# Sums of squares of the heads: one float32 product replaced by two single float32r passes over a split of the squares into two parts

## The chip, the cores and the metric

The kernel runs on one core of a Trainium2 chip. The metric is the device time in microseconds (us) of one execution. All runs quoted here were of the state "fast"; most executions of one kernel on this case agree within about 0.3%, though those of the changed kernel spread by 0.5%. A profile comes from one execution, and its span is some 1.8 us shorter than the time of that run (the profiled execution of the kernel before is not one of the two timed below). The ratio of two kernels is the mean time of one kernel's runs over the mean time of the other's runs of the same rounds on the same chip, so it is not quite the ratio of the medians that stand beside it.

The engines go by short names: PE is TensorE, which multiplies matrices; DVE is VectorE, ACT is ScalarE, POOL is GpSimd. PE's products lie in banks of the memory PSUM, from which ACT and DVE read them here. The granted clock is the share of TensorE's full clock that the trace records. In the listings o is a product of the attention, tp the transposes of q, kv the product of k and v, ss the sum of squares, hp a product with w_in and op one with w_out. float32r is the language's second 32-bit float type; the prediction takes it for the reduced float32 of the Trainium skill.

## The reference

```python
kv  = np.einsum('bhsd,bhse->bhde', k, v)          # batch 8, heads 8, seq 576, head_dim 64
out = np.einsum('bhsd,bhde->bhse', q, kv)
rms = np.sqrt(np.mean(out * out, axis=-1, keepdims=True) + 1e-06)
out = out / rms * g_norm
x   = out.transpose(0, 2, 1, 3).reshape(4608, 512)
h   = x @ w_in                                     # 512 -> 2048
g   = np.maximum(h, 0) + np.log1p(np.exp(-np.abs(h)))
y   = g @ w_out                                    # 2048 -> 512
```

The weights come as float64, and the kernel converts them to float32 itself.

## The kernel before

Two heads share the 128 partitions. Per pair of heads the attention has three stages: `stage_turn` transposes q and forms kv, `stage_out` forms the rows o and their squares sq, and `stage_squares` sums the squares of a head with a product by a block of ones.

```python
def stage_out(u):
    ...
    for h in range(2):                                      # two halves of 288 tokens
        o = ps_a.tile([P, HS], F32, tag="a", name="o")
        nc.tensor.matmul(o, lhsT=kv_diag[u % 2], rhs=qT[:, h * HS:(h + 1) * HS], start=True, stop=True)
        sq = att.tile([P, HS], F32, tag="sq", name="sq")    # two buffers
        nc.scalar.activation(sq, o, func=AF.Square)
        nc.vector.tensor_scalar(out=x_of(b, p, h), in0=o, scalar1=g_col, scalar2=None, op0=ALU.mult)
        sqs[u, h] = sq

def stage_squares(u):
    b, p = divmod(u, NP)
    for h in range(2):
        ss = ps_a.tile([P, HS], F32, tag="a", name="ss")
        nc.tensor.matmul(ss, lhsT=block, rhs=sqs.pop((u, h)), start=True, stop=True)
        nc.vector.tensor_scalar(out=mss[b][:, h, p], in0=ss, scalar1=1.0 / D, scalar2=EPS, ...)
```

The dense part runs in "slots". A slot is one product hp of w_in with its softplus (Abs, Exp and Ln on ACT, four instructions on DVE), then what an agenda deals to this slot of the attention of a later batch, then in three slots of four a quarter of an output tile (op).

```python
for s in range(SLOTS):                        # 16 slots a block of 384 tokens, 12 blocks
    if n < n_blocks:
        mm1(n, s)                             # hp and softplus
    for f, a in agenda.pop(n * SLOTS + s, []):
        f(*a)                                 # squares of pair p-1 and turn of p, or out of p
    if n > 0 and s % 4 < 3:
        i, part = divmod(s // 4 * 3 + s % 4, PARTS)
        mm2(n - 1, i, part)                   # op
```

Of the kernel before, what the change touches and what calls it, by code (L numbers as in the profile page):

```python
# [7 lines left out]

F32 = mybir.dt.float32
U32 = mybir.dt.uint32  # L10
AF = mybir.ActivationFunctionType
ALU = mybir.AluOpType
PSUM = bass.MemoryType.PSUM
# [6 lines left out]
def kernel(  # L20
# [7 lines left out]
    moe_w_out: bass.AP,  # L28
    out: bass.AP,
):  # L30
    """Per batch and pair of heads: kv = k^T v, x^T = kv^T q^T (features on partitions, so that it is
    the moving operand of the next product), the mean of squares over a head by a product with a
    block of ones, which leaves it on every row of the head. Then per block of NT tokens:
    g = softplus(w_in^T x^T), out = g^T w_out. Products and sums are float32; weights that come as
    float64 (their bits in 64-bit integers) are rounded to it here. The attention of the batches
    ahead is dealt out over the slots of the block products."""
    nc = tc.nc
    B, H, S, D = q.shape
    d_model, d_ff = moe_w_in.shape
    n_tokens = out.shape[0]  # L40
    assert (B, H, S, D, d_model) == (8, 8, 576, 64, 512) and n_tokens == B * S
    NP = H // 2                      # pairs of heads
    KD, KF = d_model // P, d_ff // P
    J = 6                            # tokens on one partition of q, k and v
    R = S // J                       # partitions of q, k and v
    HS = S // 2                      # half of a batch's tokens: one bank of PSUM
    JH = J // 2
    NT = 384                         # tokens of a block
    SLOTS = KF
    GB = 2                           # batches whose x^T lies in one tile  # L50
    BPT = GB * S // NT               # blocks of such a tile
    n_blocks = n_tokens // NT

    ctx.enter_context(tc.manual_schedule())
# [10 lines left out]
    w_out_t = const.tile([P, KF, d_model], F32, name="w_out_t")  # L65
    ident = const.tile([P, P], F32, name="ident")
    block = const.tile([P, P], F32, name="block")
    g_col = const.tile([P, 1], F32, name="g_col")
    kv_diag = [const.tile([P, P], F32, name=f"kv_diag{i}") for i in range(2)]

# [2 lines left out]
    def load(u):  # L73
        if u >= B * NP:
            return
        b, p = divmod(u, NP)
        tiles = []
        for n, src in (("q", q), ("k", k), ("v", v)):
            # q and k are stationary operands: the pair's 128 features lie together for each j
            t = qkv.tile([R, 2, J, D] if n == "v" else [R, J, 2, D], F32, tag=n, name=f"{n}_t")  # L80
            pair = src[b, 2 * p:2 * p + 2].rearrange("h (r j) d -> r h j d", j=J)
            if n == "v":
                nc.sync.dma_start(out=t, in_=pair)
            else:
                for e in range(2):
                    nc.sync.dma_start(out=t[:, :, e], in_=pair[:, e])
            tiles.append(t)
        loaded[u] = tiles
# [3 lines left out]
    conv_pool = tc.tile_pool(name="conv", bufs=2)  # L92
    conv = conv_pool.__enter__()
    raws = {}
    CHUNKS = 2 * KF                  # a weight's columns (w_in) or rows (w_out) of one kf

    def weight(c):
        """DRAM and SBUF views of chunk c, d_model values on a partition."""
        kf = c % KF
        if c < KF:  # L100
            words = moe_w_in.bitcast(U32) if wide else moe_w_in
            n = words.shape[1] // KF
            return (words[:, kf * n:(kf + 1) * n].rearrange("(a p) f -> p a f", p=P),
                    w_in_t[:, :, kf * P:(kf + 1) * P])
        words = moe_w_out.bitcast(U32) if wide else moe_w_out
        return words[kf * P:(kf + 1) * P].rearrange("(a p) f -> p a f", p=P), w_out_t[:, kf:kf + 1]
# [10 lines left out]
            out=raws[c].rearrange("p n two -> p (n two)").rearrange("p (a f) -> p a f", a=src.shape[1]), in_=src)  # L117

    def convert(c):
        """float64 -> float32, from the words hi (sign, exponent, 20 bits of mantissa) and lo.  # L120

        t: hi's value in float32: the exponent's top bit and its low seven stay, the three between
        only tell the range. p: t's power of two with its sign. So the value is t + lo 2^-52 p,
        which one addition rounds. m is 1 inside float32's normal range, 0 below it, huge above."""
        if not wide:
            return
        raw = raws.pop(c)
        lo, hi = raw[:, :, 0], raw[:, :, 1]
        t, p, h = (conv.tile([P, d_model], U32, tag=n, name=f"c_{n}") for n in "tph")
        lf, m = (conv.tile([P, d_model], F32, tag=n, name=f"c_{n}") for n in ("lf", "m"))  # L130
        tf, pf = t.bitcast(F32), p.bitcast(F32)
        nc.scalar.activation(lf, lo, func=AF.Copy, scale=2.0 ** -52)  # L132
        nc.vector.tensor_scalar(out=h, in0=hi, scalar1=0x7FFFFFFF, scalar2=None, op0=ALU.bitwise_and)  # L133
        nc.vector.tensor_scalar(out=t, in0=hi, scalar1=3, scalar2=0x3FFFFFF8,
                                op0=ALU.logical_shift_left, op1=ALU.bitwise_and)
        nc.vector.scalar_tensor_tensor(out=t, in0=hi, scalar=0xC0000000, in1=t,
                                       op0=ALU.bitwise_and, op1=ALU.bitwise_or)
        nc.vector.tensor_scalar(out=p, in0=t, scalar1=0xFF800000, scalar2=None, op0=ALU.bitwise_and)
        nc.gpsimd.tensor_scalar(out=m, in0=h, scalar1=float((1023 + 128) << 20), scalar2=3e38,  # L139
                                op0=ALU.is_ge, op1=ALU.mult)  # L140
        nc.vector.scalar_tensor_tensor(out=m, in0=h, scalar=float((1023 - 126) << 20), in1=m,  # L141
                                       op0=ALU.is_ge, op1=ALU.add)
        nc.gpsimd.tensor_tensor(out=lf, in0=lf, in1=pf, op=ALU.mult)  # L143
        nc.gpsimd.tensor_tensor(out=lf, in0=lf, in1=tf, op=ALU.add)  # L144
        _, dst = weight(c)
        a = dst.shape[1]
        nc.gpsimd.tensor_tensor(out=dst, in0=lf.rearrange("p (a f) -> p a f", a=a),  # L147
                                in1=m.rearrange("p (a f) -> p a f", a=a), op=ALU.mult)
        fetch(c + 3)
# [14 lines left out]
        nc.vector.memset(t, 0.0)  # L164
    for e in range(2):
        nc.vector.memset(block[e * D:(e + 1) * D, e * D:(e + 1) * D], 1.0)

    xTs, mss = {}, {}
    qTs, sqs = {}, {}

    def stage_turn(u):
        """q^T and the block-diagonal kv of a pair of heads."""
        b, p = divmod(u, NP)
        if p == 0:
            mss[b] = att.tile([P, 2, NP, HS], F32, tag="ms", bufs=1, name="ms")
# [25 lines left out]
        return xTs[b // GB][:, p, c:c + HS]  # L201

    def stage_out(u):
        """The attention's rows times g, and their squares."""
        b, p = divmod(u, NP)
        qT = qTs.pop(u)
        for h in range(2):
            o = ps_a.tile([P, HS], F32, tag="a", name="o")
            nc.tensor.matmul(o, lhsT=kv_diag[u % 2], rhs=qT[:, h * HS:(h + 1) * HS], start=True, stop=True)  # L209
            sq = att.tile([P, HS], F32, tag="sq", name="sq")  # L210
            nc.scalar.activation(sq, o, func=AF.Square)
            nc.vector.tensor_scalar(out=x_of(b, p, h), in0=o, scalar1=g_col, scalar2=None, op0=ALU.mult)  # L212
            sqs[u, h] = sq

    def stage_squares(u):
        b, p = divmod(u, NP)
        for h in range(2):
            ss = ps_a.tile([P, HS], F32, tag="a", name="ss")
            nc.tensor.matmul(ss, lhsT=block, rhs=sqs.pop((u, h)), start=True, stop=True)  # L219
            nc.vector.tensor_scalar(out=mss[b][:, h, p], in0=ss, scalar1=1.0 / D, scalar2=EPS,  # L220
                                    op0=ALU.mult, op1=ALU.add)

# [13 lines left out]
    def mm1(n, kf):  # L236
# [5 lines left out]
        for kd in range(KD):  # L242
            nc.tensor.matmul(hp, lhsT=w_in_t[:, kd, kf * P:(kf + 1) * P], rhs=xT[:, kd, c:c + NT],  # L243
                             start=(kd == 0), stop=(kd == KD - 1))
        # softplus(h) = max(h, 0) + log1p(u), u = exp(-|h|);
        # log1p(u) = ln(w) + (u - (w - 1)) with w = 1 + u rounded, which keeps small u whole
        # once what the table gives for ln(1) is taken off.
        u = tmp.tile([P, NT], F32, tag="u", name="u")
        nc.scalar.activation(u, hp, func=AF.Abs)  # L249
        nc.scalar.activation(u, u, func=AF.Exp, scale=-1.0)  # L250
        ln = tmp.tile([P, NT], F32, tag="ln", name="ln")
        nc.scalar.activation(ln, u, func=AF.Ln, bias=1.0)  # L252
        w = tmp.tile([P, NT], F32, tag="w", name="w")
        nc.vector.tensor_scalar(out=w, in0=u, scalar1=1.0, scalar2=None, op0=ALU.add)  # L254
        nc.vector.scalar_tensor_tensor(out=w, in0=w, scalar=1.0, in1=u, op0=ALU.subtract, op1=ALU.subtract)  # L255
        nc.vector.scalar_tensor_tensor(out=ln, in0=hp, scalar=0.0, in1=ln, op0=ALU.max, op1=ALU.add)  # L256
        nc.vector.scalar_tensor_tensor(out=gs[n][:, kf], in0=ln, scalar=ln_one, in1=w,  # L257
                                       op0=ALU.subtract, op1=ALU.subtract)

    PARTS = 4                        # slots over which one tile of 128 tokens is summed  # L260

    def mm2(n, i, part):
        if part == 0:
# [8 lines left out]
            r0 = n * NT + i * P  # L272
            nc.sync.dma_start(out=out[r0:r0 + P], in_=ot)

    # the first batch
    for t in range(NP + 2):
        if t < NP:
            stage_turn(t)
# [7 lines left out]
        for p in range(NP):  # L286
            stage_norm(0, h, p)

    # the other batches, by slot
    agenda = {}  # L290

    def at(slot, f, *a):
        agenda.setdefault(slot, []).append((f, a))

    for b in range(1, B):
        # the slot where the first block that takes from batch b starts, less the slots of its work
        due = (b * S // NT) * SLOTS
        s0 = max(due - (28 if b % GB else 30), 0)
        for p in range(NP):
# [4 lines left out]
        for i in range(2 * NP):  # L304
            at(s0 + 2 * NP + (i + 1 if b > 1 else i), stage_norm, b, i // NP, i % NP)

    AHEAD = NP + 2                   # chunks of the weights that are ready before the first block
    for c in range(AHEAD, CHUNKS):
        at((c - AHEAD) * SLOTS // (CHUNKS - AHEAD), convert, c)

# [44 lines left out]
```

## Time and profile before

| | before |
|---|---|
| time, median of 2 runs | 1355.41 us (1354.22 to 1356.6) |
| span of the profiled run | 1353.7 us |
| PE, DVE, ACT busy | 1166.8, 775.3, 418.8 us |
| stretch bound by the conversion of the weights | about 34 to 306 us |
| stretch bound by PE | 306 us to the end |
| first product o after the conversion | 313.99 us |

The last line is a mark: everything before it is the first batch and the conversion, everything after it ("the rest") is bound by PE, 1353.7 - 314.0 = 1039.7 us.

### The profile page before, as it was taken

The page shows a single profiled execution, that of the slowest core. Times are in us where ns is not written, and L with a number is a line of the kernel's source. Part 1 is how long each engine was busy: PE and PEld are TensorE (multiplying, and loading weights), DVE is VectorE, ACT ScalarE, POOL GpSimd, SP SyncE. Part 2 cuts the span into 40 slices and gives each one's busy share as a digit, 9 for nine tenths or more (in the row PEclk, how much of TensorE's full clock was granted, in tenths as well). Part 3 has the DMA queues.
Part 4 walks back from the last instruction along what each step waited for, and adds up shares of the span by engine and source line. Part 5 has one row for each costly group of instructions (what it writes and reads, how often), then busy time and mean ns, then how long its engine had stood idle before and what let it go on. Part 6 is the DMA issues. An engine that isn't in the chain of part 4 may idle for free.

```text
span 1353.7 us, 10306 instructions
## 1 busy us (share of the span) xinstructions
PE 1166.8 (86%) x3520; PEld 642.1 (47%) x3520; DVE 775.3 (57%) x1254; ACT 418.8 (31%) x798; POOL 214.2 (16%) x134
## 2 busy tenths in 40 slices
PE   6164524259999999999999999999999999999998
PEld 4042312125555555555555555555555555555543
DVE  4888989885384476343674584335844754343320
ACT  2222222113433343333432433334233333233320
POOL 5658776770000000000000000000000000000000
PEclk8667766579999999999999999999999999999999
DMA  9324311102202200012012100121020000000000
GB/s 212 86 73 115 89 62 46 62 16 66 55 8 61 61 8 8 16 46 68 16 35 60 35 9 8 30 65 35 8 61 9 8 16 9 8 8 8 16 8 24
DMA packets 98582, 55.21 MB, mean 41 GB/s; under 512 B 77536, under 2 KB 91872, under 8 KB 98528
## 3 DMA queue, kind: packets, MB, share of 16 engines
q1 hardware_dynamic: 98528, 54.54, 14.9%
q8 instruction: 28, 0.46, 0.1%
q14 instruction: 26, 0.21, 0.0%
HBM read 45.09 MB, written 9.44 MB: 40 GB/s over the span
## 4 chain that ended last, share of the span: by engine, by line
PE 76%; DVE 10%; POOL 8%; ACT 3%; issue 1%; DMA 1%; SPq 1%; POOLq 0%; ACTq 0%
PE op L267 36%; PE hp L243 34%; POOL c_m L139 4%; PE kv L192 3%; DVE ms L229 2%; PE o L209 2%; DVE w L255 2%; DVE w L254 2%; POOL c_lf L143 2%; POOL c_lf L144 1%; DVE g L257 1%; DVE c_m L141 1%; ACT qT L187 1%; ACT u L250 1%; ACT u L249 1%
## 5 line engine op out<-in xcount | busy, mean ns | idle before, releaser
L243 PE MATMUL hp<-xT,w_in_t 128*128 128x384 f32 x1536 | 550.7, 507 | 111.3 <-DVE ln L256 85.2
L267 PE MATMUL op<-w_out_t,g 128*128 128x512 f32 x1152 | 516.1, 592 | 0.0
L243 PEld LDWEIGHTS hp<-xT,w_in_t 128*128 128x128 f32 x1536 | 303.7, 199 | 358.4 <-issue 98.6
L254 DVE TENSOR_SCALAR w<-u 128x384 f32<-128x384 f32 x192 | 85.9, 448 | 468.1 <-ACT u L250 468.1
L267 PEld LDWEIGHTS op<-w_out_t,g 128*128 128x128 f32 x1152 | 217.0, 190 | 238.1 <-issue 211.9
L249 ACT ACTIVATE u<-hp 128x384 f32<-128x384 f32 x192 | 93.9, 489 | 580.5 <-PE hp L243 580.4
L257 DVE SCALAR_TENSOR_TENSOR g<-ln,ln_one,w 128x384 f32<-128x384 f32 x192 | 124.9, 650 | 14.5 <-POOL w_out_t L147 0.7
L255 DVE SCALAR_TENSOR_TENSOR w<-w,u 128x384 f32<-128x384 f32 x192 | 122.3, 637 | 6.7
L229 DVE RECIPROCAL ms<-ms 128x288 f32<-128x288 f32 x64 | 124.5, 1945 | 2.2 <-ACT ms L224 2.2
L256 DVE SCALAR_TENSOR_TENSOR ln<-hp,ln 128x384 f32<-128x384 f32 x192 | 105.9, 551 | 0.9
L252 ACT ACTIVATE ln<-u 128x384 f32<-128x384 f32 x192 | 100.5, 524 | 6.1
L250 ACT ACTIVATE u<-u 128x384 f32<-128x384 f32 x192 | 100.4, 523 | 6.1
L139 POOL TENSOR_SCALAR c_m<-c_h 128x512 f32<-128x512 uint32 x32 | 70.4, 2201 | 81.7 <-DVE c_h L133 80.6
L192 PE MATMUL kv<-v_t,k_t 96*128 96x128 f32 x384 | 58.7, 310 | 21.6 <-ACT qT L187 16.2
L192 PEld LDWEIGHTS kv<-v_t,k_t 96*128 96x128 f32 x384 | 52.7, 217 | 26.6 <-ACT qT L187 20.6
L132 ACT ACTIVATE c_lf<-raw 128x512 f32<-128x512 uint32 x32 | 21.2, 667 | 127.3 <-POOL w_out_t L147 84.7
L209 PE MATMUL o<-qT,kv_diag 128*128 128x288 f32 x128 | 40.8, 445 | 21.1 <-DVE kv_diag L195 20.4
L143 POOL TENSOR_TENSOR c_lf<-c_lf,c_p 128x512 f32<-128x512 f32 x32 | 56.5, 1767 | 2.6
L271 ACT COPY ot<-op 128x512 f32<-128x512 f32 x36 | 21.1, 586 | 109.1 <-PE op L267 109.1
L184 PE MATMUL tp<-ident,q_t 96*128 96x96 f32 x192 | 24.3, 266 | 24.9 <-DVE xT L212 18.9
L209 PEld LDWEIGHTS o<-qT,kv_diag 128*128 128x128 f32 x128 | 25.8, 207 | 34.1 <-DVE kv_diag L195 22.3
L219 PE MATMUL ss<-sq,block 128*128 128x288 f32 x128 | 37.7, 419 | 4.4 <-DVE xT L212 2.9
(33 smaller groups left out, 469.9 us busy)
## 6 DMA issues: line engine op xcount, KB each, us to landing
q_t<-in_q_dram SPq DMA_DIRECT2D x64, 144.0 KB, 3.1
k_t<-in_k_dram SPq DMA_DIRECT2D x64, 144.0 KB, 3.5
v_t<-in_v_dram SPq DMA_DIRECT2D x32, 288.0 KB, 3.8
out_dram<-ot SPq DMA_DIRECT2D x36, 256.0 KB, 2.0
raw<-in_moe_w_in_dram SPq DMA_DIRECT2D x16, 512.0 KB, 4.1
raw<-in_moe_w_out_dram SPq DMA_DIRECT2D x16, 512.0 KB, 3.3
g_col<-in_g_norm_dram SPq DMA_DIRECT2D x2, 0.2 KB, 3.1
```

The source lines that it names most:

```text
L139: nc.gpsimd.tensor_scalar(out=m, in0=h, scalar1=float((1023 + 128) << 20), scalar2=3e38, op0=ALU.is_ge, op1=ALU.mult)
L192: nc.tensor.matmul(kv, lhsT=k_t[:, j].rearrange("r h d -> r (h d)"), rhs=v_t[:, :, j, :], start=(j == 0), stop=(j == J - 1))
L229: nc.vector.reciprocal(r, r)
L243: nc.tensor.matmul(hp, lhsT=w_in_t[:, kd, kf * P:(kf + 1) * P], rhs=xT[:, kd, c:c + NT], start=(kd == 0), stop=(kd == KD - 1))
L249: nc.scalar.activation(u, hp, func=AF.Abs)
L250: nc.scalar.activation(u, u, func=AF.Exp, scale=-1.0)
L252: nc.scalar.activation(ln, u, func=AF.Ln, bias=1.0)
L254: nc.vector.tensor_scalar(out=w, in0=u, scalar1=1.0, scalar2=None, op0=ALU.add)
L255: nc.vector.scalar_tensor_tensor(out=w, in0=w, scalar=1.0, in1=u, op0=ALU.subtract, op1=ALU.subtract)
L256: nc.vector.scalar_tensor_tensor(out=ln, in0=hp, scalar=0.0, in1=ln, op0=ALU.max, op1=ALU.add)
L257: nc.vector.scalar_tensor_tensor(out=gs[n][:, kf], in0=ln, scalar=ln_one, in1=w, op0=ALU.subtract, op1=ALU.subtract)
L267: nc.tensor.matmul(op, lhsT=gs[n][:, kf, i * P:(i + 1) * P], rhs=w_out_t[:, kf], start=(kf == 0), stop=(kf == KF - 1))
```

## The change

A pass is one run of the operand through PE; the prediction counts four for a float32 product and one for a float32r product. The change splits each square into hi, a slightly scaled copy that ACT writes as float32r, and lo, the rest (the square less hi), and sums both in single float32r passes into the same bank: two passes instead of four. To make room, sq and the softplus's w are cut to one buffer. With two buffers of sq and the rest of the change as it is, the program does not fit: the conversion's pool wants 32 KiB of each partition and finds 31.53.

```diff
+    block_r = const.tile([P, P], F32R, name="block_r")
 ...
+    nc.vector.tensor_copy(block_r, block)
 ... stage_out:
-            sq = att.tile([P, HS], F32, tag="sq", name="sq")
+            sq = att.tile([P, HS], F32, tag="sq", bufs=1, name="sq")
             nc.scalar.activation(sq, o, func=AF.Square)
             nc.vector.tensor_scalar(out=x_of(b, p, h), in0=o, ...)
-            sqs[u, h] = sq
+            hi = att.tile([P, HS], F32R, tag="hi", name="hi")
+            lo = att.tile([P, HS], F32R, tag="lo", name="lo")
+            nc.scalar.activation(hi, sq, func=AF.Copy, scale=1.0 - 2.0 ** -13)
+            nc.vector.tensor_tensor(out=lo, in0=sq, in1=hi.bitcast(F32), op=ALU.subtract)
+            sqs[u, h] = hi, lo
 ... stage_squares:
-            nc.tensor.matmul(ss, lhsT=block, rhs=sqs.pop((u, h)), start=True, stop=True)
+            for i, part in enumerate(sqs.pop((u, h))):
+                nc.tensor.matmul(ss, lhsT=block_r, rhs=part, start=(i == 0), stop=(i == 1))
 ... mm1:
-        w = tmp.tile([P, NT], F32, tag="w", name="w")
+        w = tmp.tile([P, NT], F32, tag="w", bufs=1, name="w")
```

The other lines of the diff define the name F32R and drop comments.

More of the change, by code (lines that the diff above doesn't have):

```diff
@@ L10 @@
 U32 = mybir.dt.uint32
+F32R = mybir.dt.float32r
 AF = mybir.ActivationFunctionType
```

## The prediction

> **What bounds the kernel now.** I read the page first, then a table of busy time by stretch, the waits, the chain that ended last, and the timeline of single slots. A "slot" is one turn of the kernel's inner loop: one product of w_in (8 records of hp), whatever attention work is dealt to it, and in three slots of four 8 records of the product with w_out (op).
>
> The page's strip of 40 slices (34 us each) shows two regimes. DVE and POOL are full and PE half empty, at a reduced granted clock, for the first eight or nine slices; after that PE is full and POOL is done.
>
> ```profile
> PE   6164524259999999999999999999999999999998
> DVE  4888989885384476343674584335844754343320
> POOL 5658776770000000000000000000000000000000
> PEclk8667766579999999999999999999999999999999
> ```
>
> The table by stretch puts numbers on it:
>
> ```profile
> core 0: us, PE busy (x) PEld busy (x) DVE busy (x) ACT busy (x) POOL busy (x), PEclk, DMA share, GB/s
> 34.00:306.00 272.00, 116.43 (x288) 65.97 (x289) 240.42 (x283) 61.98 (x109) 197.02 (x119) 0.67 0.24 68
> 306.00:1308.00 1002.00, 987.77 (x3048) 541.22 (x3046) 516.31 (x934) 345.29 (x666) 0.00 (x0) 1.00 0.10 28
> ```
>
> From 34 to 306 us the weights are converted; DVE (240 of 272 us) and POOL (197) take turns. From 306 to 1308 PE is busy 988 of 1002 us at full clock. The other 14 us are nearly all one wait, in the waits of that stretch: 18 kv products that wait for a copy of q^T on ScalarE.
>
> ```profile
> PE kv L192 <- ACT qT L187: 14.2, 18, 0.8
> ```
>
> So in the long stretch only PE's own path counts: time taken out of PE helps unless such a wait eats it, and time added on ACT or DVE hurts only where PE comes to wait for it.
>
> **What the Trainium skill says.** (1) "FP8 and Floating Point Precision", section TensorE Precision Notes: true float32 takes four passes, reduced float32 is read cut to about 22 bits. With "TensorE: Matmul & The Clock Gate", section Back-to-back issue gap (N/2.4 + 2.5 ns warm), a float32 product of 288 columns should take 4 x 122.5 = 490 ns. The trace agrees: two ss products begin at 443.79 and the next work at 444.76, 0.97 us. (A float32 product leaves two records, so 128 records are 64 products.) (2) "PSUM — Partial Sum Buffer", section on bank collisions: a scheduler adds a dependency between any two instructions of different engines on one bank, reads included. The trace agrees: the scaling xT (DVE) waits for the square sq (ACT) of the same bank, though it does not use it. (3) "SBUF — State Buffer", section two separate sides: DVE instructions with two SBUF inputs and GpSimd exclude each other. The trace agrees in that the two-input product xT (L231) took 0.88 us once beside POOL work and 0.46 us without.
>
> **The change part by part.** Removed: 64 float32 products ss (128 records, four passes). Added: 128 float32r products, which I take as one pass each; 64 copies hi on ACT; 64 subtractions lo on DVE; one small copy at the start, hidden. Moved: sq has one buffer instead of two, so the square of a pair's second half waits until lo of the first half has read sq. In the order of the built program the scaling of the second half waits for that square. So what ran as sq, sq on ACT beside x, x on DVE becomes a zigzag: x0, lo0 (DVE), sq1 (ACT), then hi1 (ACT) beside x1 (DVE), then lo1 (DVE), and only then the last of the four ss passes. The single buffer of w costs nothing: DVE alone writes and reads it, in order.
>
> Passes: 4 x 122.5 = 0.49 us per pair of heads instead of 0.97, so 0.48 saved per pair, on paper 32 x 0.48 = 15 us. Most of it is not paid out. Here is a slot from the timeline (start us, duration, engine, line):
>
> ```profile
> 440.24 1.13 PE L209 MATMUL o<-qT,kv_diag 128*128 128x288 f32 x4
> 441.21 2.74 PE L243 MATMUL hp<-xT,w_in_t 128*128 128x384 f32 x8
> 441.95 0.69 ACT L211 ACTIVATE sq<-o 128x288 f32<-128x288 f32 x2
> 443.63 0.94 DVE L212 TENSOR_SCALAR xT<-o,g_col 128x288 f32<-128x288 f32 x2
> 443.79 1.13 PE L219 MATMUL ss<-sq,block 128*128 128x288 f32 x4
> 443.99 0.49 ACT L249 ACTIVATE u<-hp 128x384 f32<-128x384 f32 x1 [1.35 <-PE hp L243]
> 444.76 0.66 PE L184 MATMUL tp<-ident,q_t 96*128 96x96 f32 x6
> 445.50 0.66 ACT L187 COPY qT<-tp 128x288 f32<-128x288 f32 x1
> 446.21 1.60 PE L192 MATMUL kv<-v_t,k_t 96*128 96x128 f32 x12 [0.79 <-ACT qT L187]
> ```
>
> Between the products o and ss stands only one hp (2.58 us), as the slot has no op. Today sq is long ready at 443.79, and ss starts without a wait. I listed o and what follows for all 24 pairs after 306 us: 12 have hp alone between o and ss ("short"), 12 have op and hp, 6.0 us ("long"). 9 of the short and 9 of the long are followed by transposes and kv (the 18 waits above); 3 of each are the last of their batch and are followed by op.
>
> A short pair, from the start of o as zero. DVE reaches x0 at 3.39 as now (443.63), its interval is 0.47. lo0: a DVE tensor_tensor of this shape, L231, takes 0.46, so it ends at 4.32. sq1 on ACT: 0.41 alone in this trace, with 0.05 for the hand-over, 4.37 to 4.78. Then x1 on DVE 4.82 to 5.33. hi1 on ACT: 0.44, from Exp of 384 columns at 0.52 less 96/1.2 ns, so to 5.25. lo1 5.29 to 5.75. The last ss pass ends near 5.95, against 4.52 now: PE waits, and goes on about 1.45 us later, the shorter passes already counted. If kv follows, ACT decides: Abs of this slot starts after hi1 at 5.16 instead of 3.75, so Abs, Exp, Ln and the q^T copy, and kv with them, come 1.4 us later. Both ways about +1.43: 12 x 1.43 = +17.2 us.
>
> A long pair: the same zigzag ends near 5.75, and ss begins 6.98 after o, so nothing waits. Where kv follows, the 0.48 us only lengthens the wait for the q^T copy, as that copy stands behind Abs, Exp and Ln of the slot's hp and not behind ss: gain 0. Where op follows: 3 x -0.48 = -1.4 us. After 306 us together +15.8.
>
> In the conversion, DVE is in the chain around every scaling of batch 1, as the chain in order of time shows:
>
> ```profile
> 93.44 0.94 DVE g L257
> 94.39 0.85 DVE xT L212 x2
> 95.66 1.77 POOL c_m L139
> ```
>
> The two scalings (0.93 us in the timeline) become x0, lo0, the hole for sq1, x1, lo1: 0.46 + 0.46 + 0.46 + 0.46 + 0.46 = 2.3 us, so +1.37 for each of four pairs, +5.5 us, handed on to POOL, which stands idle for c_h there. For batch 0, the first two pairs hide behind loads and a present wait of sq for ss (a buffer of sq), which the change removes; the later two have some slack beside POOL. I put +1.5 on it. Conversion +7.
>
> Sum: 1355.4 + 15.8 + 7.0 = 1378 us, 1.7% slower.
>
> **The rivals.** (a) The gain is paid out: PE is the bound, half of ss goes, and DVE and ACT have room (57% and 31% busy). Then 24 x 0.48 = 11.5 us fall away, at best 1344. For it speaks the full PE row; against it the 18 waits for q^T, which ss does not end, and the 12 short pairs. (b) The zigzag does not reach PE, because the short pairs' hp is long enough. That needs lo1 before 3.55, and x0 alone ends at 3.86. Only the conversion's cost would stay: about 1361. (c) The delays are larger: lo is locked out by GpSimd work in the conversion, each hand-over costs 0.1 us more, the weight loads of the single passes (0.19 us in the trace) stand bare after a wait, or ACT's delay reaches the next slots. 0.5 us more per short pair and 1 us more per pair in the conversion give 1392. (d) float32r is no cheaper than float32. No row of this trace tells. It would add 0.49 us to the 15 pairs at most that are not held by q^T: up to 1386.
>
> **Range and chances.** The zigzag's steps are durations of this trace, so rival (a) is unlikely. The least certain terms are the conversion (0 to 14 us) and the waits per short pair (1.0 to 1.9). That gives 1366 to 1390. The line of 2% lies at 1382.5, 4.5 us above my number, with some 8 us of spread. Faster 0.03, same 0.66, slower 0.31.
>
> **What would show it.** Each step has its place in the new profile: ss records 128 of about 0.12 us spacing, PE busy down by some 15 us; new waits of PE at ss for lo (DVE) in exactly 12 slots after 306 us, or of kv for q^T grown from 0.8 to about 2 us in the 9 short ones and to about 1.3 in the long ones; sq1 about 0.8 us behind sq0's end or more, waiting for lo; DVE up by 64 x 0.46 = 29 us, ACT by 28; the PE-bound stretch beginning at about 313 instead of 306. It would be wrong if the short pairs start kv on time, if the passes are not single, or if the conversion ends where it did.

## The result, and the profile after

The changed kernel took 1389.0 us (median of 2 runs, 1385.43 and 1392.57) against 1355.41: ratio 1.0248, 95% interval 1.0218 to 1.0278. The profiled run had a span of 1383.7 us. In a later job the same kernel took 1386.77 us (4 runs), ratio 1.0227. So it is slower by somewhat more than 2%.

The table of busy time by stretch, kernel after. The columns are start and end, length, busy us of each engine with its instruction count, the mean granted clock, the DMA share and GB/s.

```profile
320.00:1320.00 1000.00, 969.13 (x2971) 528.71 (x2970) 526.47 (x960) 360.22 (x699) 0.00 (x0) 0.99 0.10 28
```

From 320 to 1320 us PE is idle for 31 of 1000 us, where it was idle for 14 of 1002 before. And the granted clock is 0.99, where it was 1.00: a small digit that turns out to matter. The waits from 312 us on, kernel after (who waited, for whom, us in total, times, longest):

```profile
ACT sq L214 <- DVE lo L220: 42.9, 24, 1.8
...
PE kv L195 <- ACT qT L190: 17.1, 18, 1.2
...
PE ss L228 <- ACT hi L219: 6.9, 12, 0.6
...
PE ss L228 <- DVE lo L220: 5.8, 12, 0.5
```

The three waits of PE are the old one for the q^T copy and two new ones, each in 12 places: the 12 short pairs. (kv does not read q^T. In the built program 22 of the 32 kv are given the PSUM bank of the transposes before them, so they wait until ACT has copied these out.) The first line is the zigzag: 24 times ACT stands for 1.8 us with the square of the second half, until lo of the first half has read the only buffer. A short pair in the timeline of the kernel after (start us, duration, engine, line, and in brackets the idle time before):

```profile
451.84 1.13 PE L212 MATMUL o<-qT,kv_diag 128*128 128x288 f32 x4
...
453.54 0.39 ACT L214 ACTIVATE sq<-o 128x288 f32<-128x288 f32 x1
453.97 0.44 ACT L219 ACTIVATE hi<-sq 128x288 fp32r<-128x288 f32 x1
...
455.23 0.51 DVE L215 TENSOR_SCALAR xT<-o,g_col 128x288 f32<-128x288 f32 x1
455.66 0.45 DVE L220 TENSOR_TENSOR lo<-sq,hi 128x288 fp32r<-128x288 f32 x1
...
456.20 0.41 ACT L214 ACTIVATE sq<-o 128x288 f32<-128x288 f32 x1 [1.79 <-DVE lo L220]
456.64 0.44 ACT L219 ACTIVATE hi<-sq 128x288 fp32r<-128x288 f32 x1
456.65 0.52 DVE L215 TENSOR_SCALAR xT<-o,g_col 128x288 f32<-128x288 f32 x1 [0.54 <-ACT sq L214]
456.99 0.47 ACT L258 ACTIVATE u<-hp 128x384 f32<-128x384 f32 x1
457.12 0.46 DVE L220 TENSOR_TENSOR lo<-sq,hi 128x288 fp32r<-128x288 f32 x1
...
457.63 0.40 PE L228 MATMUL ss<-lo,block_r 128*128 128x288 f32 x1
...
457.87 0.66 PE L187 MATMUL tp<-ident,q_t 96*128 96x96 f32 x6
...
458.49 0.66 ACT L190 COPY qT<-tp 128x288 f32<-128x288 f32 x1
...
459.20 1.60 PE L195 MATMUL kv<-v_t,k_t 96*128 96x128 f32 x12 [0.67 <-ACT qT L190]
```

Read it against the slot of before in the prediction, with o as zero. The last lo ends at 5.74 us (predicted 5.75), Abs of this slot starts at 5.15 instead of 3.75 (5.16), and kv starts at 7.36 instead of 5.97 (7.41). The steps fell where they were put.

What was not foreseen is in the following lines: the same table for 3.4 us stretches around another short pair of the kernel after, whose o started at 353.25.

```profile
358.00:361.41 3.41, 2.10 (x15) 1.70 (x16) 2.80 (x6) 2.47 (x6) 0.00 (x0) 1.00 0.01 2
361.41:364.80 3.39, 3.39 (x11) 2.03 (x10) 1.67 (x5) 0.21 (x1) 0.00 (x0) 0.53 0.58 132
364.80:368.20 3.40, 3.40 (x10) 1.61 (x9) 0.00 (x0) 0.00 (x0) 0.00 (x0) 0.96 0.49 131
```

After a stretch in which PE was busy only 2.10 of 3.41 us, the granted clock is halved for 3.41 us although PE is full again, and those 3.41 us of work lose about 1.7 us. The trace's record of the clock has four such half-clock windows in the PE-bound rest of this run, and none in that of the kernel before. Four of them are 6.8 us.

The sum for the profiled runs is then closed: the first o after the conversion came at 321.58 us instead of 313.99 (+7.6), and the rest took 1062.1 us instead of 1039.7 (+22.4). Of the 22.4, the short pairs are 9 x 1.39 (kv) + 3 x 1.51 (the op after ss, which starts 6.03 instead of 4.52 us after o) = +17.0, the three long pairs before op are 3 x -0.44 = -1.3, and the four half-clock windows are +6.8: together 22.5.

### The profile page after: what moved, and what is told of

It is laid out like the page before. It is cut to its first block, busy times and chain, and to the rows that moved or that the text cites. A ratio compares the mean times of both kernels' runs of the same rounds, so it can differ in the third digit from the quotient of the medians.

```text
span 1383.7 us, 10559 instructions
## 1 busy us (share of the span) xinstructions
PE 1179.8 (85%) x3520; PEld 647.0 (47%) x3520; DVE 801.6 (58%) x1319; ACT 447.7 (32%) x862; POOL 213.8 (15%) x134
## 4 chain that ended last, share of the span: by engine, by line
PE 72%; DVE 13%; POOL 8%; ACT 5%; issue 1%; DMA 1%; SPq 1%; ACTq 0%; POOLq 0%
PE op L276 36%; PE hp L252 31%; POOL c_m L141 4%; PE kv L195 4%; DVE w L264 2%; DVE ms L238 2%; DVE w L263 2%; DVE g L266 2%; POOL c_lf L145 1%; ACT u L259 1%; PE o L212 1%; ACT u L258 1%; DVE ln L265 1%; POOL c_lf L146 1%; DVE c_m L143 1%
## 5 line engine op out<-in xcount | busy, mean ns | idle before, releaser
L195 PE MATMUL kv<-v_t,k_t 96*128 96x128 f32 x384 | 64.1, 330 | 25.1 <-ACT qT L190 20.8
L195 PEld LDWEIGHTS kv<-v_t,k_t 96*128 96x128 f32 x384 | 57.5, 234 | 30.2 <-ACT qT L190 25.2
L214 ACT ACTIVATE sq<-o 128x288 f32<-128x288 f32 x64 | 25.8, 404 | 107.0 <-DVE lo L220 96.1
L228 PE MATMUL ss<-lo,block_r 128*128 128x288 f32 x64 | 24.0, 381 | 41.1 <-DVE lo L220 39.9
L212 PE MATMUL o<-qT,kv_diag 128*128 128x288 f32 x128 | 42.2, 456 | 15.7 <-DVE kv_diag L198 15.1
L215 DVE TENSOR_SCALAR xT<-o,g_col 128x288 f32<-128x288 f32 x64 | 32.9, 514 | 18.2 <-ACT sq L214 18.1
```

The lines of the kernel that those rows point to most:

```text
L195: nc.tensor.matmul(kv, lhsT=k_t[:, j].rearrange("r h d -> r (h d)"), rhs=v_t[:, :, j, :], start=(j == 0), stop=(j == J - 1))
```

## The experiments

The theory: the time is lost because the one buffer of sq strings the two halves of a pair into a zigzag between DVE and ACT. In the conversion it lengthens DVE's chain; after it, it holds up PE directly (ss for lo) and through ACT (kv for the q^T copy behind the delayed hi), in the 12 short pairs only; and the holes it makes in PE bring half-clock windows on top. The rivals: the added work of hi and lo costs the time by itself; PE's wait for lo is all of it; the single passes are dear; the half-clock windows are accidental.

For all runs, the marks read from the PE timeline and the clock record of the one profiled execution:

| kernel | ratio to before (95%) | first o after conversion, us | rest, us | half-clock windows in the rest |
|---|---|---|---|---|
| before | 1 | 314.0 | 1039.7 | 0 |
| after | 1.0248 (1.0218 to 1.0278) | 321.6 | 1062.1 | 4 |
| e1 two buffers of sq | 1.0091 (1.0076 to 1.0106) | 319.0 | 1047.5 | 1 |
| e2 after, op first | 0.9895 (0.9878 to 0.9911) | 322.2 | 1017.8 | 0 |
| e3 before, op first | 0.9863 (0.9848 to 0.9877) | 314.1 | 1021.2 | 0 |
| e4 one pass | 0.9970 (0.9955 to 0.9985) | 314.1 | 1037.1 | 1 |
| e5 after again | 1.0227 (1.0213 to 1.0241) | 320.2 | 1063.7 | 5 |
| e6 after, waits filled | 1.0159 (1.0145 to 1.0173) | 322.9 | 1055.4 | 0 |
| e7 op first, two buffers | 0.9823 (0.9810 to 0.9837) | 320.0 | 1011.0 | 0 |
| e8 as e7, split late only | 0.9789 (0.9775 to 0.9802) | 314.3 | 1011.1 | 0 |
| e9 split in batches 0, 1 only | 1.0056 (1.0039 to 1.0073) | 323.5 | 1039.7 | 0 |
| e10 split in batches 2 to 7 only | 1.0178 (1.0162 to 1.0193) | 312.1 | 1063.7 | 5 |
| e11 work of hi and lo, unused | 1.0043 (1.0026 to 1.0059) | 319.3 | 1039.7 | 0 |
| e12 PE does not wait for lo | 1.0243 (1.0222 to 1.0264) | 321.7 | 1066.9 | 6, two of them double |

The medians were: e1 1368.19, e2 1341.76, e3 1337.12, e4 1352.05, e5 1386.77, e6 1377.68, e7 1332.58, e8 1327.70, e9 1363.99, e10 1379.86, e11 1361.02, e12 1389.65 us, each of 4 runs (e6 of 5), beside medians of before of 1355.65 (e1 to e4), 1356.38 (e5 to e8) and 1355.35 us (e9 to e12).

### e9 and e10: the two terms of the sum, each alone

```diff
+            split = b < 2          # e9;  b >= 2 in e10
 ... where not split: sq takes a buffer of the tag "hi" (two of them), no lo,
 ... and ss is the float32 product with block, as before
```

> The change in batches 0 and 1 alone (their work is done in the conversion stretch); batches 2 to 7 keep the float32 product of one square. Theory: the conversion's term of the sum by itself, +7 to 8 us, ratio 1.0055; the first o after the conversion near 321.5 us instead of 314.0. Rival (DVE has room there, 1 us in 9 idle): below 1.002.

> The change in batches 2 to 7 alone; batches 0 and 1 keep the float32 product. Theory: the PE-bound term by itself, 16 us and some half-clock windows (4 to 8 of 1.7 us): ratio 1.016 to 1.022, and the conversion ends at 314 us as before. With e9 it makes up the whole. Rival (the passes saved on PE show): below 1.01.

e9 gave 1.0056, and its rest is 1039.7 us, to the digit that of before: the split of the early batches costs only in the conversion. e10 gave 1.0178, with the conversion over at 312.1 us and all of the loss in the rest. Together they are 2.3%, as much as the whole in e5. So about a quarter of the loss is the conversion's and three quarters are PE's.

### e11: the added work without the waits

```diff
 ... before, with
+            hi = att.tile(...); lo = att.tile(...)
+            nc.scalar.activation(hi, sq, func=AF.Copy, scale=1.0 - 2.0 ** -13)
+            nc.vector.tensor_tensor(out=lo, in0=sq, in1=hi.bitcast(F32), op=ALU.subtract)
             sqs[u, h] = sq         # still the operand of the float32 product; two buffers
```

> The kernel before, with hi and lo computed and then not used: ACT and DVE do all the added work, sq has two buffers, PE still multiplies sq in float32 and waits for no hi or lo. Theory: PE does not see it after 306 us (ss waits for sq alone), only the conversion pays 4 to 5 us: ratio 1.0035. Rival (the work is the cost): about 1.02.

It gave 1.0043, and the rest is again 1039.7 us. In the rest, ACT and DVE do all that the change adds, and PE's time does not move by a tenth of a microsecond. The rival "the work is the cost" falls for the PE-bound part. In the conversion the work does cost, 5.3 us by the first o. This kernel also has the single buffer of w, which thereby is cleared.

### e1: two buffers of sq

```diff
-            sq = att.tile([P, HS], F32, tag="sq", bufs=1, name="sq")
+            sq = att.tile([P, HS], F32, tag="sq", name="sq")
 ... room: no tile "block"; the ones are set in kv_diag[0], copied to block_r, and cleared
```

> The change with two buffers of sq again (room made by building the block of ones in a tile that is zeroed afterwards). Theory (zigzag over one buffer): sq1 and hi1 no longer wait for lo0, so ACT's Abs starts on time in the short pairs; only the four DVE steps x0, lo0, x1, lo1 in a row remain, lo1 ending near 5.25 us after o. Then kv comes 0.6 us later than before in the 9 short pairs with kv, and PE 1.0 us later in the 3 without: about +7 us after 306 us, +5 us in the conversion, ratio to before about 1.009 to 1.013. Rival (the added work of hi and lo costs the time, not the wait): as the change, 1.025.

It gave 1.0091. In the short pairs kv starts 6.53 us after o (predicted 6.6; 7.36 with one buffer) and the op after ss at 5.37 (6.03). More than half of the loss goes away with one buffer of 1152 bytes per partition: of the 1.39 us by which kv came late in these pairs, the missing buffer made 0.83. What stays is the row of four DVE steps, which still ends after PE arrives.

### e12: PE spared the wait for lo, ACT not

```diff
-            for i, part in enumerate(sqs.pop((u, h))):
+            hi, lo = sqs.pop((u, h))
+            for i, part in enumerate((hi, hi)):
```

> The change with hi multiplied twice instead of hi and lo (the sums come out nearly double, so the result is wrong by a factor of about 0.7, on purpose): lo is computed, and sq1 still waits for it through the one buffer, but PE does not. Theory: in the 9 short pairs followed by kv nothing is gained, as kv waits for the q^T copy that stands behind the delayed sq1 and hi1 on ACT, and 0.4 us in the 3 others: ratio 1.022 to 1.024. Rival (PE's wait for lo is the cost): about 1.008.

The result is wrong as intended (relative error 0.21). The ratio stayed at 1.0243: kv still starts 7.36 us after o. In the pair whose o started at 451.95:

```profile
459.31 2.15 PE L195 MATMUL kv<-v_t,k_t 96*128 96x128 f32 x12 [1.02 <-ACT qT L190]
```

PE's direct wait for lo, the line that catches the eye in the list of waits, is not what sets the time in the nine pairs followed by kv. There it is ACT, held up by the zigzag, that delivers the q^T copy late. This run also had more half-clock windows than the others, six, two of them of double length.

### e4: what the saved passes are worth

```diff
 ... before, with
-            sq = att.tile([P, HS], F32, tag="sq", name="sq")
+            sq = att.tile([P, HS], F32R, tag="sq", name="sq")
-            nc.tensor.matmul(ss, lhsT=block, rhs=sqs.pop((u, h)), start=True, stop=True)
+            nc.tensor.matmul(ss, lhsT=block_r, rhs=sqs.pop((u, h)), start=True, stop=True)
```

> The kernel before with the square written as float32r and a single pass (no hi, no lo; coarser, so the result may be off by some 1e-4). PE saves 0.72 us per pair. Theory: of the 24 pairs after 306 us the 18 that are followed by kv give it back as a longer wait for the q^T copy, so 6 x 0.72 = 4 us, ratio 0.997. Rival (the saved passes are paid out in full and only the split's work costs): 24 x 0.72 = 17 us, ratio 0.987.

It gave 0.9970, as the theory said, and within the accepted error, though it multiplies squares written as float32r and has no lo. A short pair in the PE timeline of this kernel:

```profile
439.66 1.13 PE L213 MATMUL o<-qT,kv_diag 128*128 128x288 f32 x4
...
442.91 0.72 PE L223 MATMUL ss<-sq,block_r 128*128 128x288 f32 x2
443.61 0.89 PE L188 MATMUL tp<-ident,q_t 96*128 96x96 f32 x6
445.63 1.60 PE L196 MATMUL kv<-v_t,k_t 96*128 96x128 f32 x12 [1.12 <-ACT qT L191]
```

The transposes start 3.95 us after o instead of 4.52, and kv starts at 5.97 as before: the wait for the q^T copy has grown by what ss gave up. The rest of the profiled run, 1037.1 us, contains one half-clock window, at 1011.94 us after such a pair; without its 1.67 us it would be 4.3 us shorter than before, the 6 x 0.72 of the theory. A window can thus appear without any zigzag, after a pair whose only added hole is the longer wait for the q^T copy. So even a quarter of the passes at no added work is worth 0.3% in this schedule.

### e5 and e6: the half-clock windows

e5 is the change unaltered. e6 puts useless passes where PE waits, in the 12 short pairs:

```diff
             hi, lo = sqs.pop((u, h))
+            for _ in range((4 if h == 0 else 2) if short else 0):
+                nc.tensor.matmul(ss, lhsT=block_r, rhs=hi, start=True, stop=True)
+            for _ in range(4 if short and h == 0 else 1):
                 nc.tensor.matmul(ss, lhsT=block_r, rhs=hi, start=True, stop=False)
                 nc.tensor.matmul(ss, lhsT=block_r, rhs=lo, start=False, stop=True)
```

> The change itself, unaltered, as partner of e6. Ratio to before 1.025. Theory (part of the loss is half-clock windows of 3.4 us in which the granted TensorE clock drops to 0.5 after a short pair): the times of the runs differ by some us, and in the profiled one the count of such windows after 320 us, at 1.7 us each, makes up what the PE-bound stretch loses beyond about 16 us.

> The change with useless passes put into PE's waits of the 12 short pairs: hi of the first half is multiplied five times, the sum of the first half is done four times, hi of the second half three times, each time starting the sum anew, so the result stays. 12 more passes of 0.12 us per short pair, 1.5 us, nearly all where PE now waits. Theory (the idle PE brings the half-clock windows): none after 320 us, so 5 to 10 us faster than e5 although PE does more, ratio about 1.018 to 1.021. Rival (the windows have nothing to do with these waits, or don't matter): as e5 or up to 3 us slower, ratio 1.025 to 1.027.

e6 was faster than e5 by 9.1 us in the medians, with intervals of the ratio that do not overlap, though PE does 12 more passes per short pair. (Its ratio, 1.0159, lies below the 1.018 to 1.021 that was expected, as e5's own came out at 1.0227 and not 1.025.) Its table by stretch, from 320 us on, has the full clock back:

```profile
320.00:1320.00 1000.00, 982.99 (x3133) 547.19 (x3132) 529.62 (x966) 361.53 (x702) 0.00 (x0) 1.00 0.10 28
```

Its rest is 1055.4 us, that is 15.7 more than before: the waits of the prediction (+15.8) and nothing else; kv starts 7.36 us after o in its short pairs too. e5 had five windows and a rest 8.3 us above e6's, after had four and 6.7: 1.67 us each. The half-clock windows are a consequence of the holes in PE, and the rival falls.

Which of the 12 pairs gets a window differs from run to run, but the clock records hold a rule for it. In each profile all changes of the granted clock fall on one grid with a step of 3.41 us. In the profiles of after, e5 and e10, which have the same short pairs, the 14 windows follow just those 14 short pairs with kv whose o starts 1.79 to 2.76 us after a step of the grid. The 13 others with kv, at 0.83 to 1.76 us, have none, nor have the 9 followed by op. So the number of windows depends on where the holes happen to lie on the grid. In e6 three pairs with kv lie in that band as well, and filled they have no window. PE's recorded busy share of the step before a window (0.53 to 0.70) does not separate the cases by itself: steps with 0.64 had none after them. The reason for the band stays open.

### e2 and e3: no short pairs

```diff
-            for f, a in agenda.pop(n * SLOTS + s, []):
-                f(*a)
             if n > 0 and s % 4 < 3:
                 i, part = divmod(s // 4 * 3 + s % 4, PARTS)
                 mm2(n - 1, i, part)
+            for f, a in agenda.pop(n * SLOTS + s, []):
+                f(*a)
```

> The change with the op products of a slot issued ahead of the slot's attention work, so that every ss after the conversion has op and hp (6 us) between it and its o. Theory: no pair is short, no PE wait for lo or for a late q^T copy, no half-clock windows after 320 us, and the shorter passes pay 0.48 us for each of 24 pairs: about 11 us less than e3, plus 7.6 us in the conversion: about 4 us below e3, ratio to before about 0.993. Rival (the single passes or the added ACT and DVE work are dear in themselves): above e3, ratio above 1.

> The kernel before with the same reordering (op ahead of the attention work), the partner of e2. All theories: the wait of kv for the q^T copy shrinks from 0.79 us to about 0.5 as the copy no longer stands behind Abs, Exp and Ln of the slot: about 5 us less, ratio 0.996.

e3 was better than expected, 0.9863 instead of 0.996: the wait of kv disappeared (kv starts 0.50 us after the transposes, the time these take), as in this order the banks of PSUM are handed out otherwise: in the built program 4 of the 32 kv take the bank that the q^T copy on ACT has to empty, where 22 did before. I had assumed that the dependency stays. The rest shrank by 18.5 us.

e2 missed. All waits for lo are gone, as expected, and it is faster than before; but it is 0.3% above e3, not below. The conversion costs +8.1 us against e3, as expected, but the rest is only 3.4 us shorter instead of 11. A line of its timeline says why:

```profile
452.44 1.60 PE L195 MATMUL kv<-v_t,k_t 96*128 96x128 f32 x12 [0.53 <-DVE ms L229]
```

kv waits for ms, the eviction of ss on DVE. The zigzag ends before PE comes to ss, but it has held up Abs on ACT and with it the four DVE instructions of the softplus, behind which ms stands. It does so in the pairs whose o lies in a slot without op, where the softplus of that slot's hp begins only with o itself; in the others the slot's op gives ACT and DVE a lead of 3.4 us, and 0.42 us is paid out (11.98 us from one o to the next, 12.40 in e3).

### e7 and e8: the repaired version

e7 is e2 with e1's two buffers. e8 adds:

```diff
 ... stage_out, after the scaling:
+            if b < 2:
+                sqs[u, h] = (sq,)      # float32 product with block_r read as float32
+                continue
 ... stage_squares: such an sq is multiplied once, with block_r.bitcast(F32)
```

> e2 (op ahead of the attention work) with two buffers of sq. In e2 the zigzag, though no longer in front of ss, held up Abs and the four DVE steps of the next hp, and with them the eviction of ss, whose bank kv needs: 0.5 us of waiting of PE in the pairs followed by kv after a slot without op. Theory: with two buffers DVE is only 0.9 us later and kv hardly waits, so nearly 24 x 0.45 us are paid out against e3, less 5 us in the conversion: ratio about 0.982, below e3 at 0.986. Rival (the added ACT and DVE work eats the gain in any order): at or above e3.

> e7 with the split only for the batches that are dealt out after the conversion (2 to 7); batches 0 and 1 keep the float32 product, as DVE is the bound there and PE is not. Theory: the 5 us of the conversion vanish: about 1327 us, ratio 0.979, faster than both kernels.

e7 gave 0.9823 and e8 0.9789, 1327.7 us, both correct. From 320 to 1320 us e8's profile has PE busy 1000.00 of 1000 us. Its rest is 10.1 us shorter than e3's, where 24 x 0.44 = 10.6 was on offer. So the idea of the change does pay, 0.75% from e3 to e8 (0.9789 / 0.9863), once PE is given something to do while hi and lo are made, and where PE and not DVE is the bound.

## Why the prediction was right or wrong

The forecast was 1378 us, 1366 to 1390; the two runs gave 1389.0 in the median, and 1386.8 in e5. The direction and the mechanism held, and the range holds the median near its upper end, though not the slower of the two runs (1392.57). That it holds the median is in part luck, as its width had been given to other terms. But I gave "within 2%" more than twice the chance (0.66) that I gave to what happened (0.31), because one term was missing.

- **Conversion, +7.0.** Measured +7.6 in the profile of after and +6.2 in e5, by the first o; alone (e9) +9.5 in the profile. The zigzag there, from x0 to the next c_h, took 2.26 us (96.82 to 99.08) instead of 0.85 (94.31 to 95.16): +1.41, against +1.37 in the working. Part by part: from POOL's last step on the sixth of the 32 chunks of weights to that on the 21st, a stretch that holds batch 1's four pairs and none of batch 0's, after, e5 and e9 each take 152.0 us instead of 146.76, so +5.3 against the +5.5 of the working. e1 and e11 take 149.5 and 149.8 there: more than half of this term is the added work itself, and only the other part the buffer. Up to the sixth chunk the three lose 2.6, 1.2 and 2.9 us, against +1.5; but e10, which leaves batch 0 unsplit, comes there 1.2 us earlier than before, so this part is not measured better than to a us or two.
- **Short pairs, 12 x 1.43 = +17.2.** Measured 9 x 1.39 + 3 x 1.51 = +17.0. Right, and for the reason given: e12 shows that ACT's lateness sets it where kv follows, and e1 that 0.83 of the 1.39 us come from the one buffer and the rest from the two added DVE steps.
- **Long pairs, -1.4.** Measured -1.3; those followed by kv start kv at 9.41 us after o as before. Right; e4 shows the same with no split at all.
- **Single passes.** In a long pair the transposes start 7.51 us after o instead of 7.95. Counted from 6.98, where PE has finished hp, the four passes take 0.53 us instead of 0.97, so float32r is a single pass at the expected pace. Rival (d) fell.
- **The step that failed: the clock after 306 us was taken as full.** The prediction read "at full clock" from the table of before and carried it over, though it put 12 holes into PE. The half-clock windows cost 6.7 us in the profiled run and about 8 in e5; e6 takes them away, and 1055.4 - 1039.7 = 15.7 is what is left of the rest, against 15.8 in the working. 1378.2 + 6.7 is 1384.9, and the profiled run took 1385.4. The spread that I gave to "conversion" and "waits per short pair" belonged to this term.
- **Signs that I named badly.** PE's busy time did not fall by 15 us but rose from 1166.8 to 1179.8: a record of a pass that stands alone is longer than its share of PE (0.40 us recorded, 0.13 us from one to the next where they follow closely), and the slow windows add more. And the wait of kv in the short pairs did not grow to 2 us but is 0.67, as PE already waits at ss; it is the start of kv that moved. The starts are the better sign. ACT rose by 28.9 us (28 named), DVE by 26.3 (29 named).

Of the rivals, (a) "the gain is paid out" holds only after the order of the slot and the buffers are mended, and (c) "the delays are larger" came nearest in its number, 1392, but hardly by the routes that it named. One of them shows in batch 0 of after, where three of the eight lo took 0.83 to 1.36 us beside POOL work instead of 0.46, 1.9 us more in all; batch 1's eight took 0.44 to 0.46, with no POOL work beside them. Why the two runs of after differ by 7 us is consistent with about four more windows (their mean granted clocks are 0.922 and 0.918), but that run has no trace, so this is argued, not shown.

## What to carry to other kernels

Before shortening an instruction on the bound engine, ask what that engine does next: if it then waits for another engine, the saving is only a longer wait (e4). When operands are now made in more steps, see how much time stands between their source and their use in each place of the schedule, not on average, and count the buffers that the steps pass through: one missing buffer turned two parallel halves into a zigzag and made 0.83 of the 1.39 us that were lost in each short pair followed by kv (e1). And a hole in TensorE can cost more than its length, as it can halve the clock for the work that comes after it; the granted clock of a stretch belongs into the estimate.

## What the Trainium skill lacked or had wrong

- "TensorE: Matmul & The Clock Gate", the table of goals ("Why this matters for your kernels"), asks to avoid idle gaps of over about 3 us. Here a half-clock window followed a stretch in which PE was never idle for as much as 1 us at a time and was recorded busy for 2.10 of 3.41 us. The section "A second HAM failure mode" of the same page does say that short idle times between groups bring the clock down; it gives no share of busy time. Filling the holes removed all four or five windows of a run (e6). The same page's reckoning that a throttled time costs half its length agrees: 3.41 us at half clock cost 1.67 us per window here.
- "FP8 and Floating Point Precision", TensorE Precision Notes, does not name float32r or its pace. Here a float32r product of 288 columns took 0.13 us from one to the next, a float32 product 0.485 us.
- "PSUM — Partial Sum Buffer", the section on bank collisions, explains why a scheduler orders an ACT and a DVE reader of one bank. No page says what that order does with a chain: here the scaling on DVE waited 0.54 us for a square that it does not use, once in each of the 24 pairs after 312 us.
